# The first layer's stores moved to ScalarE's queue, and the next chunk's load one step earlier

## Chip, cores and metric
One core of a Trainium2 chip runs the whole program. The metric is the device time of one execution in microseconds (us), here the median of several runs. The program uses TensorE (PE: matrix multiplications), ScalarE (ACT) and VectorE (DVE) for everything elementwise, SyncE (SP) for nearly all transfers and GpSimd (POOL) for a few.

## What is computed
Three parts in a row: channel attention, which becomes a 256 x 256 matrix `a` that multiplies `v`, and two feed-forward layers on 6080 tokens with 256 channels and 2048 hidden ones.

```python
def _attn_ref(q, k, v, tau):
    qn = q / (np.linalg.norm(q, axis=1, keepdims=True) + 1e-06)
    kn = k / (np.linalg.norm(k, axis=1, keepdims=True) + 1e-06)
    s = kn.transpose(0, 2, 1) @ qn / tau
    ...
    return (v @ a).astype(np.float32)        # a: softmax of s over its last axis

def _moe_ref(x, w_in, w_out):                # first layer
    r = np.maximum(x @ w_in, 0.0)
    return ((r * r) @ w_out).astype(np.float32)

def _moe2_ref(x, w_in, w_out):               # second layer
    h = x @ w_in
    g = h * np.clip(h + 3.0, 0.0, 6.0) / 6.0
    return (g @ w_out).astype(np.float32)
```

The attention matrix is folded into the first layer's `w_in`, so after a head of about 100 us the kernel consists of two layers. Each multiplication takes three passes (high x high, high x low, low x high parts).

## The kernel before
**Chunks and steps.** The tokens are cut into six chunks of two blocks of 508 or 506 columns. A layer (`ph` 0 or 1) goes through its chunks (`c` 0 to 5), and a chunk through eight steps: four slices of the hidden channels (`u`), two halves each (`p`). `i` counts the steps over both layers, 0 to 95; `at` is the step within the chunk, 0 to 7 (`LAST`). In the trace chunk 1 of the first layer (i = 8 to 15) begins at 157.9 us, chunk 2 at 240.8, chunk 3 at 328.2, chunk 4 at 415.4, chunk 5 at 502.4, the second layer at 589.6; a step takes about 10.4 us.

**A step** (`step`, L669) multiplies by the input weights into PSUM (`mul`, L678, tile `s`), and ACT and DVE turn the sums into hidden values (copies `m`, `u`; values `h`; their high and low parts `g`). Between these multiplications TensorE does those by the output weights that belong to the step before (`out_mms`, run by `run_outs`, L662, tile `y`), 24 a step in portions (`pop`). The copy `m` of a step (L768) has to be done before the third group of `mul` (L783) may add into the same bank, and a copy `u` (L784) before the next (L790).

**Output tiles** (`y_done`, L645). With the last slice of a chunk its four sums (two blocks, two halves of the channels) are complete. As the output multiplications run one step late, this falls into step 0 of the next chunk: two of them in the middle of the step, two at its end. ACT copies each from PSUM into a tile `y` (L659; two buffers, `bufs=2`), and a store moves it to memory: to `scratch` (tensor `y` in the trace's names, so `y<-y`) for the first layer, to `outT` for the second. So the third eviction of a chunk needs the buffer of the first, whose store has to have landed.

**The next chunk's data** (`load_data`, L382) are two loads into the tile `blk`, which has one buffer. From it ACT and DVE make the operands `b`: the `lane`, filled by `add_lane` from the chunk's third step on, and at `LAST` for the rest; its last reader of `blk` is in the chunk's last step. The first layer loads from `vT`, the second from `scratch`; the data of the second layer's first chunk are loaded in chunk 5 of the first.

**Weights of the second layer** are converted during chunks 1 to 5 of the first layer by a planner (`background`): each task has a due step and is worked off in small pieces between a step's instructions (`beside`). A task loads raw words (`words`, L263, tile `w`), converts them on ACT (L135, L136: `ct<-w`, `cv<-w`) and DVE, and stores high and low parts (`keep`, L334: `w2h`, `w2l`, `o2h`, `o2l`).

**Order.** From i = 8 on each engine and queue takes its instructions in program order. SP's queue therefore holds, one behind the other as the program came to them: the words' loads, the stores of `keep`, the stores of `y`, the loads of `blk`. An issue waits on SP until its data are ready, and what is behind it waits too.

Of the kernel before, what the change touches and what calls it, by code (L numbers as in the profile page):

```python
# [59 lines left out]
def tile_channel_attention_then_two_ffn(  # L60
# [13 lines left out]
    PE, ACT, DVE, SP = nc.tensor, nc.scalar, nc.vector, nc.sync  # L74
# [125 lines left out]
    def run(fs):  # L200
        for f in fs:
            f()
# [16 lines left out]
    def add_task(name, load, due, alone=False, size=5):  # L219


        at = len(tasks)
        while at > 2 and tasks[at - 1].due > due:
            at -= 1
        tasks.insert(at, Task(name, load, due, alone, size))
        ensure_loads()
# [18 lines left out]
    def need(name):  # L245
        assert name in finished or any(t.name == name for t in tasks), name
        while name not in finished:
            background()
# [71 lines left out]
    def add_out_1(u, due):  # L320
        def parts(a):
            if (0, u) not in o_ops:
                o_ops[0, u] = [oop.tile([P, 4, C], F32R, tag="o" + t, name="o" + t) for t in "hl"]
            return [t[:, a:a + 2] for t in o_ops[0, u]]
        for a in (0, 2):
            add_task(("o", u) if a else None, convert_split(out_cut(w_out_1, u, a), 2, lambda a=a: parts(a)), due)
# [55 lines left out]
    def load_data(ph, c):  # L382
        r = blocks_tile("blk")
        data[ph, c] = r
        start, n = chunks[c]
        for g in range(2):
            src = vT[:, start + g * n:start + (g + 1) * n] if ph == 0 else scratch[c][:, g * n:(g + 1) * n]
            SP.dma_start(out=r[:, 2 * g:2 * g + 2, :n], in_=src.rearrange("(h p) t -> p h t", p=P))
# [16 lines left out]
    def add_lane(ph, c, slots, due):  # L405
        assert not lane
        b_ops.setdefault((ph, c), {})
        lane.extend(data_prep(data[ph, c], chunks[c][1], slots, new_slot(ph, c)))
        lane_due[0] = due

    def add_data(name, ph, c, slots, due):
        b_ops.setdefault((ph, c), {})
        add_task((name, ph, c), lambda: data_prep(data[ph, c], chunks[c][1], slots, new_slot(ph, c)), due,
                 size=2 * len(slots) + 2 * ("sums" in slots))
# [12 lines left out]
    def attn_w(u):  # L427

        if u == 1:

            ps = [psy.tile([P, 512], F32, tag=f"y0{dh}", name="aw") for dh in range(2)]
        else:
            ps = [bank([P, 512]) for _ in range(2)]

        def product(dh, eh):
            return lambda: PE.matmul(ps[dh], e_sb[dh][:, eh], w1[u][:, eh], start=(eh == 0), stop=(eh == 1))  # L436

        r = blocks_tile("wblk")
        data["w", u] = r

        def take(dh):
            def f():
                ACT.activation(out=r[:, dh:4:2], in_=ps[dh].rearrange("p (g f) -> p g f", g=2),
                               func=AF.Copy, scale=rsum[:, dh:dh + 1])
            return f
        return [product(dh, eh) for dh in range(2) for eh in range(2)], [take(dh) for dh in range(2)]
# [13 lines left out]
    with tc.tile_pool(name="qk", bufs=4) as qkp, tc.tile_pool(name="at", bufs=1) as atp:  # L460
# [53 lines left out]
        for i, (rest, j, g) in enumerate(pieces):  # L514
            if i:
                load_piece(i + 3)
            t = loaded[i]
# [86 lines left out]
    def in_1_steps(u):  # L604
        r = data["w", u]
        w_ops[0, u] = new_ops(wop, "w")
        ops = lambda: w_ops[0, u]
        if u < PLAIN:
            return split_slots(r, ops, RAW + OTHER)
        return split_slots(r, ops, RAW) + weight_sums(r) + split_slots(r, ops, SUMS)  # L610
# [8 lines left out]
    def out_mms(ph, c, u, p, g):  # L619


        n = chunks[c][1]
        wh, wl = o_ops[ph, u]
        first, last = (u, p) == (0, 0), (u, p) == (NU - 1, 1)
        mms = []

        def one(e, b, w, j, of, part, start, stop):
            def f():
                x = g[of][:, part, :n]
                if (ph, c, b, e) not in y_ps:  # L630
                    y_ps[ph, c, b, e] = psy.tile([P, HT], F32, tag=f"y{b}{e}", name="y")
                PE.matmul(y_ps[ph, c, b, e][:, :n], w[:, j, e * P:(e + 1) * P], x, start=start, stop=stop)  # L632
            return f


        for k, (i, b) in enumerate(((1, 1), (0, 1), (0, 0), (1, 0))):
            j = 2 * i + p
            for e in range(2):
                mms.append((one(e, b, wh, j, (i, b), 0, first and k % 2 == 0, False), None))
                mms.append((one(e, b, wl, j, (i, b), 0, False, False), None))  # L640
                mms.append((one(e, b, wh, j, (i, b), 1, False, last and k % 2 == 1),
                            (ph, c, b, e) if last and k % 2 else None))
        return mms

    def y_done(ph, c, b, e, last=False):  # L645
        start, n = chunks[c]
        if ph == 0 and c not in scratch:
            scratch[c] = dram.tile([C, 2 * HT], F32, tag="y1", name="y1")
        scale = 1.0 if ph == 0 else 1.0 / 6.0
        t = yp.tile([P, HT], F32, tag="y", name="y")  # L650
        y = y_ps[ph, c, b, e]
        dst = scratch[c][:, b * n:] if ph == 0 else outT[:, start + b * n:]
        dst = dst[e * P:(e + 1) * P]
        cuts = (0, n // 2, n) if last else (0, n)
        for k, (i, j) in enumerate(zip(cuts, cuts[1:])):
            if k:
                DVE.tensor_scalar(out=t[:, i:j], in0=y[:, i:j], scalar1=scale, scalar2=None, op0=ALU.mult)
            else:
                ACT.activation(out=t[:, i:j], in_=y[:, i:j], func=AF.Copy, scale=scale)  # L659
            SP.dma_start(out=dst[:, i:j], in_=t[:, i:j])  # L660

    def run_outs(outs, n):  # L662
        for _ in range(min(n, len(outs))):
# [148 lines left out]
    LAST = 2 * NU - 1  # L812
# [18 lines left out]
    for i, (ph, c, u, p) in enumerate(order):  # L831
        at = i % (LAST + 1)
        nxt = (ph, c + 1) if c + 1 < NCHUNK else (1, 0) if ph == 0 else None
        if ph == 0 and c == 0:
            if i == 0:
                add_out_1(1, 3)
            elif p == 1 and u + 1 < NU and u:
                add_out_1(u + 1, i + 2)
        if (ph, c) == (0, 1) and at == 0:
            end = i  # L840
            for x, f in [(x, f) for x in range(NU) for f in (add_in_2, add_out_2)]:
                end += DUE[f is add_out_2]
                f(x, end)
        if nxt and at == (1 if i > LAST else 3) + 1:
            add_lane(*nxt, FIRST, i - at + LAST)
        if at == 0:
            assert not lane
        if ph == 0:
            need(("w", ph, u))
            if PLAIN <= u and c == 0:  # L850
                need(("t", 0, 0))
            if c == 1 and u < PLAIN:
                need(("s", u))
        outs = []
        if not prev:
            need(("w1", 1))
            products, take = attn_w(1)
            outs = [(f, None) for f in products]
        else:
            if prev[0][0] == 0 and prev[0][1] == 0:  # L860
                need(("o", prev[0][2]))
            outs = out_mms(*prev[0], prev[1])
        if i == MANUAL_FROM:
            phase[0] = 2
            ctx.enter_context(tc.manual_schedule())

        if nxt and at == LAST:
            add_lane(*nxt, REST, i + 1)
        g, carry = step(i, ph, c, u, p, before, outs, carry)
        before = []  # L870
        if nxt and at == (1 if i > LAST else 3):
            load_data(*nxt)
        if ph == 0 and c == 0 and p == 0 and u + 1 < NU:
            need(("w1", u + 1))
            if u == 2:
                need(("s", 0))
            if u:
                products, before = attn_w(u + 1)
                run(products)
            else:  # L880
                before = take
            add_task(("w", 0, u + 1), lambda x=u + 1: in_1_steps(x), i + 2)
        if ph == 0 and c == 0 and u < PLAIN:
            if p == 0:
                add_data("t", 0, 0, ("sums", 5, 4, 3, 6), i + 2)
            else:
                add_weight_sums(u, SUMS_DUE)
        if ph == 0 and c == NCHUNK - 1 and p:
            fetch_2("w", u)
        if prev and prev[0][0] == 0 and prev[0][1] == NCHUNK - 1 and prev[0][3]:  # L890
            fetch_2("o", prev[0][2])
        prev = ((ph, c, u, p), g)
# [38 lines left out]
```

## Time and profile before
| | us |
|---|---|
| runs | 1091.4, 1099.7, 1102.7; median 1099.7 |
| profiled execution | 1099.3 |
| its span in the profile | 1097.5 |

| engine | busy us | share of the span |
|---|---|---|
| PE | 1071.4 | 98% |
| DVE | 900.3 | 82% |
| ACT | 648.8 | 59% |

The share of PE is an average over all stages, and matmuls that run at a lower clock count as busy too. So the stages have to be read one by one: how long each chunk takes, and at which granted clock. The rows of the section before the prediction give these, and the timelines of SP and ACT around the chunk ends.

### The profile page before, as it was taken

Reading aid. Unit: us, or ns where it says so; the run is one execution under the profiler, and the core shown is the slowest. Engines: PE = TensorE matmul, PEld = TensorE weight load, DVE = VectorE, ACT = ScalarE, POOL = GpSimd, SP = SyncE. Lnnn points to the kernel's source line nnn. Section 1 sums busy time; section 2 is a strip of 40 time slices with the busy share of each in tenths; the row PEclk is TensorE's granted clock in tenths of the full one; section 3 lists DMA queues with packets and bytes.
Section 4 is the critical chain, followed back from the end, with each engine's and each line's share of the span. In section 5 each row is a group of like instructions: output and inputs, shape, how many; then the busy total and the mean of one; then the engine's idle time right before and its main releaser. Section 6 shows DMA issues by size and latency. Waiting matters only on the chain.

```text
span 1097.5 us, 12762 instructions
## 1 busy us (share of the span) xinstructions
PE 1071.4 (98%) x4576; PEld 866.2 (79%) x4576; DVE 900.3 (82%) x1547; ACT 648.8 (59%) x1126; POOL 9.3 (1%) x22
## 2 busy tenths in 40 slices
PE   8999999999999999999999999999999999999998
PEld 6757778887887887888788888888888888888886
DVE  5899987886986886887677898898898898898785
ACT  5588966665566565667556545545545545555443
POOL 0000000000000000000101000000000000000000
PEclk9899999999999999999999999999999999999999
DMA  9523213114023014112544101100100100100001
GB/s 354 216 77 108 85 39 115 67 42 130 29 89 122 29 65 127 39 48 106 175 169 155 66 1 42 36 1 34 43 1 31 46 1 26 51 1 21 18 1 39
DMA packets 33568, 78.03 MB, mean 71 GB/s; under 512 B 3296, under 2 KB 16864, under 8 KB 33504
## 3 DMA queue, kind: packets, MB, share of 16 engines
q1 hardware_dynamic: 31200, 65.68, 17.7%
q0 software_dynamic: 2304, 11.54, 3.0%
q8 instruction: 36, 0.59, 0.2%
q14 instruction: 28, 0.23, 0.1%
HBM read 53.22 MB, written 23.99 MB: 70 GB/s over the span
## 4 chain that ended last, share of the span: by engine, by line
PE 88%; DVE 5%; DMA 3%; ACT 2%; issue 1%; SPq 1%; ACTq 0%; DVEq 0%
PE y L632 46%; PE s L683 40%; PE s L436 1%; DMA y<-y 1%; DVE accq L111 1%; DMA w<-w_in_dram 1%; DVE acck L111 1%; DMA blk<-vT_dram 1%; PE sc L505 1%; DMA blk<-y 1%; DVE g L108 0%; ACT sq L532 0%; DVE wl L108 0%; DMA w<-w_out_dram 0%; DVE b L108 0%
## 5 line engine op out<-in xcount | busy, mean ns | idle before, releaser
L632 PE MATMUL y<-g,oh 128*128 128x506 f32 (+1 forms) x1536 | 512.2, 394 | 0.3 <-ACT oh L105 0.3
L683 PE MATMUL s<-b,wh 128*128 128x506 f32 (+1 forms) x1348 | 423.3, 395 | 11.6 <-ACT u L105 5.5
L108 DVE TENSOR_TENSOR g<-h,g 128x506 fp32r<-128x506 f32 (+1 forms) x384 | 261.8, 682 | 108.3 <-ACT g L105 99.0
L632 PEld LDWEIGHTS y<-g,oh 128*128 128x128 f32 x1536 | 291.4, 190 | 66.2 <-ACT oh L105 0.8
L683 PEld LDWEIGHTS s<-b,wh 128*128 128x128 f32 x1348 | 253.9, 189 | 74.0 <-ACT u L105 7.9
L632 PE MATMUL y<-g,ol 128*128 128x506 f32 (+1 forms) x768 | 304.2, 396 | 0.3 <-DVE ol L108 0.2
L683 PE MATMUL s<-b,wl 128*128 128x506 f32 (+1 forms) x674 | 265.8, 394 | 0.6 <-DVE wl L108 0.6
L105 ACT ACTIVATE g<-h 128x506 fp32r<-128x506 f32 (+1 forms) x384 | 234.9, 622 | 27.0 <-DVE h L728 14.4
L105 ACT ACTIVATE u<-s 128x506 f32<-128x506 f32 (+1 forms) x188 | 111.6, 594 | 144.9 <-PE s L683 144.8
L632 PEld LDWEIGHTS y<-g,ol 128*128 128x128 f32 x768 | 145.7, 190 | 32.7 <-DVE ol L108 1.0
L111 DVE TENSOR_TENSOR h<-u,s 128x506 f32<-128x506 f32 (+1 forms) x188 | 127.5, 678 | 29.0 <-ACT u L105 27.7
L683 PEld LDWEIGHTS s<-b,wl 128*128 128x128 f32 x674 | 127.8, 190 | 29.6 <-DVE wl L108 1.6
L105 ACT ACTIVATE m<-s 128x506 f32<-128x506 f32 (+1 forms) x94 | 55.9, 595 | 111.8 <-PE s L683 111.4
L711 DVE SCALAR_TENSOR_TENSOR h<-r,h 128x506 f32<-128x506 f32 (+1 forms) x144 | 98.9, 687 | 4.9
L707 DVE SCALAR_TENSOR_TENSOR h<-h 128x506 f32<-128x506 f32 (+1 forms) x130 | 88.6, 681 | 1.4
L111 DVE TENSOR_TENSOR h<-m,s 128x506 f32<-128x506 f32 (+1 forms) x94 | 63.9, 680 | 15.0 <-ACT m L105 8.3
L727 ACT ACTIVATE r<-s,three 128x506 f32<-128x506 f32 (+1 forms) x48 | 32.9, 685 | 60.3 <-PE s L683 60.3
L710 DVE TENSOR_SCALAR r<-h 128x506 f32<-128x506 f32 (+1 forms) x144 | 60.5, 420 | 1.7
L108 DVE TENSOR_TENSOR b<-blk,b 128x506 fp32r<-128x506 f32 (+1 forms) x85 | 57.7, 679 | 0.0
L105 ACT ACTIVATE b<-blk 128x506 fp32r<-128x506 f32 (+1 forms) x85 | 52.5, 617 | 6.8 <-DMA blk<-vT_dram 3.5
L505 PE MATMUL sc<-q,k 128*128 128x256 f32 x192 | 47.8, 410 | 6.1 <-DMA q<-q_dram 6.1
L724 ACT ACTIVATE r<-s 128x506 f32<-128x506 f32 (+1 forms) x46 | 27.3, 594 | 43.2 <-PE s L683 42.9
(87 smaller groups left out, 478.3 us busy)
## 6 DMA issues: line engine op xcount, KB each, us to landing
w<-w_in_dram SPq DMA_DIRECT2D x16, 512.0 KB, 4.3
w<-w_out_dram SPq DMA_DIRECT2D x16, 512.0 KB, 3.8
k<-k_dram SPq DMA_DIRECT2D x10, 512.0 KB, 7.9
q<-q_dram SPq DMA_DIRECT2D x10, 512.0 KB, 8.8
blk<-vT_dram SPq DMA_DIRECT2D x8, 506.0 KB, 5.2
y<-y SPq DMA_DIRECT2D x16, 253.0 KB, 2.3
blk<-y SPq DMA_DIRECT2D x8, 506.0 KB, 5.2
outT_dram<-y SPq DMA_DIRECT2D x15, 253.0 KB, 2.1
```

Of the source, the lines that this page charges most:

```text
L105: ACT.activation(out=out, in_=in_, func=AF.Copy)
L108: DVE.tensor_tensor(out=out, in0=a, in1=b, op=ALU.subtract)
L111: DVE.tensor_tensor(out=out, in0=a, in1=b, op=ALU.add)
L436: return lambda: PE.matmul(ps[dh], e_sb[dh][:, eh], w1[u][:, eh], start=(eh == 0), stop=(eh == 1))
L505: return lambda: PE.matmul(s_ps[dh][:, :C], t["k"][:n, b, dh * P:(dh + 1) * P], t["q"][:n, b], start=first, stop=last)
L632: PE.matmul(y_ps[ph, c, b, e][:, :n], w[:, j, e * P:(e + 1) * P], x, start=start, stop=stop)
L683: PE.matmul(dst, w[:, a, rows], x, start=first and k == 0, stop=k == 2, skip_group_check=True)
L707: DVE.scalar_tensor_tensor(out=h, in0=h, scalar=0.0, in1=h, op0=ALU.max, op1=ALU.mult)
L710: DVE.tensor_scalar(out=r, in0=h, scalar1=3.0, scalar2=0.0, op0=ALU.add, op1=ALU.max)
L711: DVE.scalar_tensor_tensor(out=h, in0=r, scalar=6.0, in1=h, op0=ALU.min, op1=ALU.mult)
L724: ACT.activation(out=r, in_=x, func=AF.Relu)
L727: ACT.activation(out=r, in_=x, func=AF.Relu, bias=three)
```

## The change
Three lines. The store of an output tile of the first layer is issued by ACT, right behind ACT's own eviction; the second layer's stay on SP. From i = 8 on `load_data` is called after a chunk's first step and no longer after its second. The condition of `add_lane` is written in another way.

```diff
@@ y_done
-            SP.dma_start(out=dst[:, i:j], in_=t[:, i:j])
+            (ACT if ph == 0 else SP).dma_start(out=dst[:, i:j], in_=t[:, i:j])
@@ main loop
-        if nxt and at == (1 if i > LAST else 3) + 1:
+        if nxt and at == (2 if i > LAST else 4):
             add_lane(*nxt, FIRST, i - at + LAST)
...
         g, carry = step(i, ph, c, u, p, before, outs, carry)
         before = []
-        if nxt and at == (1 if i > LAST else 3):
+        if nxt and at == (0 if i > LAST else 3):
             load_data(*nxt)
```

## Rows read from the trace of the kernel before

**Rows 1.** Windows (us; busy PE, PEld, DVE, ACT, POOL; clock): chunk 1, chunks 2-5, next.

```profile
157.87:240.75 82.88, 82.88 (x361) 67.64 (x361) 67.25 (x114) 54.06 (x96) 0.00 (x0) 1.00 0.22 73
240.75:589.61 348.86, 338.69 (x1442) 275.98 (x1441) 266.83 (x446) 211.18 (x375) 7.42 (x14) 0.98 0.28 92
589.61:672.60 82.99, 82.99 (x362) 67.66 (x361) 72.10 (x123) 43.87 (x75) 1.16 (x3) 1.00 0.18 60
```

**Rows 2.** Waits of TensorE: us in total, times, longest us.

```profile
PE s L683 <- ACT u L105: 5.5, 3, 2.6
PE s L683 <- ACT m L105: 5.1, 2, 2.6
```

**Rows 3.** Windows, columns as in rows 1: the stretch after the first stall.

```profile
256.56:260.70 4.14, 4.14 (x11) 3.30 (x12) 2.87 (x5) 2.79 (x5) 0.00 (x0) 0.60 1.00 302
```

**Rows 4.** Timeline of ACT, chunk 2 (start us, us, instruction, idle before and releaser).

```profile
246.60 1.08 ACT L659 ACTIVATE y<-y 128x508 f32<-128x508 f32 x2
...
254.73 1.29 ACT L659 ACTIVATE y<-y 128x508 f32<-128x508 f32 x2 [4.25 <-DMA y<-y]
```

**Rows 5.** Timeline of SP, chunk 2; the last line holds four issues.

```profile
248.77 0.32 SPq L334 DMA_DIRECT2D o2l<-stl  x1
249.18 0.39 SPq L263 DMA_DIRECT2D w<-w_in_dram  x1
249.66 6.70 SPq L660 DMA_DIRECT2D y<-y  x4
```

**Rows 6.** Timeline of SP, end of chunk 2 and chunk 3.

```profile
326.22 0.42 SPq L263 DMA_DIRECT2D w<-w_in_dram  x1
...
346.51 0.32 SPq L334 DMA_DIRECT2D o2l<-stl  x1
346.88 0.42 SPq L263 DMA_DIRECT2D w<-w_in_dram  x1
347.36 0.97 SPq L388 DMA_DIRECT2D blk<-vT_dram  x2
```

**Rows 7.** Timelines of DVE and ACT, end of chunk 2 and chunk 3.

```profile
325.74 0.68 DVE L108 TENSOR_TENSOR b<-blk,b 128x506 fp32r<-128x506 f32 x1
...
350.77 0.66 ACT L135 ACTIVATE ct<-w 128x512 f32<-128x512 f32 x1
354.91 0.62 ACT L105 ACTIVATE b<-blk 128x506 fp32r<-128x506 f32 x1 [3.49 <-DMA blk<-vT_dram]
```

**Rows 8.** Issues (ns min/median/max) of L660 and L388; L660's landings at 247 to 258.

```profile
L660 SPq DMA_DIRECT2D y<-y x24: 319/320/422, 164.3 to 600.7; - x24
...
L388 SPq DMA_DIRECT2D blk<-y x12: 377/476/1205, 521.1 to 933.2; - x12
...
DMA to landing us min/median/max: 2.0/3.6/5.2
```

**Rows 9.** Timelines of ACT and PE, chunk 1, undisturbed.

```profile
163.69 1.07 ACT L659 ACTIVATE y<-y 128x508 f32<-128x508 f32 x2
165.28 0.59 ACT L724 ACTIVATE r<-s 128x508 f32<-128x508 f32 x1 [0.51 <-PE s L683]
...
167.58 1.29 ACT L659 ACTIVATE y<-y 128x508 f32<-128x508 f32 x2
168.96 0.60 ACT L105 ACTIVATE m<-s 128x508 f32<-128x508 f32 x1
...
170.83 0.63 PE L683 MATMUL s<-b,wh 128*128 128x508 f32 x2
```

**Rows 10.** Timelines of SP and ACT, chunk 5.

```profile
506.71 0.43 SPq L263 DMA_DIRECT2D w<-w_out_dram  x1
508.83 4.88 SPq L660 DMA_DIRECT2D y<-y  x4
521.10 1.72 SPq L388 DMA_DIRECT2D blk<-y  x2
...
512.08 1.28 ACT L659 ACTIVATE y<-y 128x506 f32<-128x506 f32 x2
```

## Prediction

> **What bounds the kernel now.** I read the times by stage first. In chunk 1 of the first layer TensorE is busy for the whole 82.88 us of the chunk, at a granted clock of 1.00; the next four chunks together take 348.86 us, with 338.69 busy [rows 1]. Four chunks like chunk 1 would take 4 x 82.88 = 331.52 us. So 348.86 - 331.52 = **17.3 us** is lost there, and the reader should ask where. The chunks of the second layer run like chunk 1 (the first of them 82.99, [rows 1]), so nothing of this size is lost later.
>
> The waits of TensorE come next. It waits for an ACT copy `m` twice (5.1 us) and for an ACT copy `u` three times (5.5 us), with 2.6 us as the longest of each [rows 2]: four waits of about 2.5 us, and a small one. Each costs more than its idle time: after the first, TensorE ran 4.14 us at a granted clock of 0.60 [rows 3], that is at the lower of its two levels (1.2 GHz) for most of the stretch. That is 4.14 x 0.40 = 1.7 us more, so some 4.3 us a stall, and four of them make 17.1 us, close to the 17.3.
>
> Then the reason for each, from the timelines of SP and ACT. There are two kinds.
>
> *Kind one, chunks 2 and 4: a store is late.* In chunk 2 ACT evicted two output tiles from 246.60 to 247.68, but SP issued the first store only at 249.66 [rows 4, 5]: ahead of it stood a weight store that could leave at 248.77 and a weight load at 249.18. SP takes its instructions in order. Tile `y` has two buffers, so the third eviction waits for the first store to land: ACT stood still for 4.25 us, until 254.73 [rows 4], and with it the copy `m` behind. Chunk 4 repeats it; these are the two waits for `m`.
>
> *Kind two, chunks 3 and 5: a load is late.* In chunk 3 the load of the next data stands behind a weight store that left at 346.51 and leaves at 347.36 [rows 6], and ACT's first instruction on it waits 3.49 us, to 354.91 [rows 7], with the copy `u` behind it. In chunk 5 the load leaves at 521.10 [rows 10].
>
> **The change, part by part.** *L844* is rewritten to the same value (`at` 2 or 4): nothing changes there.
>
> *L871, the load one step earlier.* Ten `load_data` calls move in program order. For the second layer nothing is issued on SP between the end of a chunk's first step and the end of its second, so its order of instructions, and its time, stay as they are. In the first layer five calls (in chunks 1 to 5) pass what the second step puts on SP: in chunk 3 one pair of weight stores and one weight load, in chunk 5 one pair of stores. In chunk 3 the load can then leave once SP has issued the weight load at 326.22 and DVE has read the old block for the last time (325.74 + 0.68 = 326.42) [rows 6, 7], so at 326.7 where it left at 347.36. There it was landed 7.6 us after it left (354.91, [rows 7]); 326.7 + 7.6 = 334.3, and ACT wants it at 351.4, right after 350.77 + 0.66. Cover: 17 us. In chunk 5 it can leave at 507.2, behind the weight load at 506.71 [rows 10]: 13.9 us before 521.10, where the wait of this kind in chunk 3 was 3.49 us. Both stalls of kind two go. Behind the load on SP stands the second step's first weight store, some 17 us later in chunk 3 (it leaves a little before the 346.51 of its pair), so nobody waits for the load's issue.
>
> *L660, 24 stores from ACT.* Six chunk ends, four stores each. In chunks 2 and 4 a store can leave as its eviction ends: 246.60 + 0.60 = 247.2 in place of 249.66. Stores of this window landed 2.0 to 5.2 us after issue, the slow one right behind the weight load [rows 8]; now it leaves 2 us ahead of that load, so I take 2.0 to 3.6 (the median): landed by 250.8. ACT reaches the third eviction at 254.73 - 4.25 = 250.5 [rows 4], plus what the two issues cost it. Both stalls of kind one go. All four gone: **-17.3 us**.
>
> The price is ACT's time. No row shows ACT issuing a transfer. The nearest are SP's issues of the same stores, 319 to 422 ns; the slowest issue on SP is 1205 ns, of a load [rows 8]. Call e an issue with its wait for the eviction ahead of it (ACT's later instructions wait behind it). Chunk 1 shows the slack, undisturbed [rows 9]. Eviction one starts at 163.69. With two issues the next instruction could start at 163.69 + 2 x 0.60 + 2e = 164.89 + 2e where it started at 165.28: 2e - 0.39 late. What follows runs without a gap to eviction three (167.58), then come two more issues: eviction three at 167.19 + 2e, the copy `m` at 168.39 + 4e, done at 168.99 + 4e. TensorE needs it at 170.83 [rows 9]. So nothing is lost up to e = (170.83 - 168.99) / 4 = **0.46 us**. I take 0.42, the slowest row of the same transfer: 0 us. Below, e = 0.32 is 0 too; above, e = 1.2 gives 4 x 1.2 - 1.84 = 2.96 us in each of six chunks.
>
> *What is late next.* In chunk 5 the earlier load meets the stores: weight load at 506.71, the two halves of the block from about 507.2 to 508.2, and store one at 508.8. If it lands in 5.2 us, as behind the weight load of chunk 2 [rows 8], it lands at 514.0; eviction three is due at 512.08 + 2e - 0.39 = 512.5 [rows 10], so it is 1.5 us late, with 4 x (0.46 - 0.42) = 0.2 us of slack left: 1.3 us of stall. If it lands in 3.6 us, nothing. Bounds 0 to 1.3 + 1.7 of slow clock = 3.0; I take the slower landing without the clock, 1.3. In chunk 3 the load has landed (334.3) before the stores leave (334.6). In chunks 2 and 4 ACT's next reader is of the weight load issued at 249.18: the like load, issued at 346.88 with a block load behind it, was there by 350.77, in under 3.9 us [rows 6, 7]; 253.1 is before ACT comes to it (`m` done at about 253.6). Nothing.
>
> *The sum.* The profiled execution took 1099.3 us (span 1097.5 and 1.8 around it); the median of the three runs is 1099.7, the lowest 1091.4. 1099.3 - 17.3 + 1.3 = **1083.3 us**; I say 1083. Whichever execution is looked at, the stalls are a matter of landings, so the lowest run may well have had two fewer; the changed kernel should then spread less.
>
> **A rule against it.** The rows show a store that was ready at 247.2 and left at 249.66 because of what stood ahead of it on SP [rows 4, 5]; its own issue is 0.32 us [rows 8]. The Trainium skill, "DMA: Bandwidth & Descriptors", section "Issuing engines are not separate DMA queues", says that transfers started by different engines end on the same 16 DMA engines and interleave, and that starting them from several engines saves only the time to start them. By that rule L660 would save no more than a few issues, and the two stalls of kind one would stay. I weigh the rows higher, since the wait ahead of the issue is on SP and not on the DMA engines; no row shows two queues' transfers of this size side by side at a store.
>
> **The rivals.**
> 1. *The stores stay late* (they share the DMA engines with the weight load and, now, the block load). For it: the 5.2 us landing. Against it: the store leaves 2 us ahead of the weight load. Half the loss stays: 1099.3 - 8.7 = 1090.6 us.
> 2. *No gain:* the new issues on ACT and collisions in chunks 3 and 5 give the whole back, or the stalls were this execution's alone. Against it: four stalls with a named cause each. About 1098 us.
> 3. *Slower:* ACT's issue is dear. It decides from the point where six stalls outweigh 17.3 us, 2.9 a chunk: e = 0.46 + 2.9 / 4 = 1.2 us without a fall of the clock, and with 1.7 us for the clock e = 0.76. At e = 1.2 with the clock: 6 x (2.96 + 1.7) = 28 us, 1099.3 - 17.3 + 28 = 1110 us. Against it: SP's issues of this very store never passed 0.42.
> 4. *The load doesn't move:* excluded for chunks 3 and 5, since SP's order shows what stands ahead of it; for chunk 1 and the second layer it holds, and is worth nothing.
>
> **Chances and range.** Forecast (all four go, 1077 to 1088): 0.63. Rival 1 (1086 to 1094): 0.17. Rival 2 (1094 to 1104): 0.12. Rival 3 (1100 to 1115): 0.08. The low end allows 6 us for runs whose head or landings are better than those of the profiled one (the lowest run before lies 8 under it); the high end takes in rival 1 and the edge of rival 2, so that 2 in 10 are left out: 1077 to 1095. A measurement of this kernel can tell about 1% from no change, so the bounds are 1088.7 and 1110.7. Faster: 0.63 and half of rival 1, 0.72. Slower: the dear part of rival 3, 0.06. Between them: the rest, 0.22.
>
> **What would show each step.** Chunks 2 to 5 at about 82.9 us each, TensorE at clock 1.00 in all of them; no wait of ACT's eviction for a store over 1.5 us; no wait of ACT for a block. ACT-queue issues of 0.3 to 0.45 us, and the copy `m` of a chunk's second step done before TensorE wants it. I am wrong if these issues take 0.6 us or more, if chunk 5 stalls as before at its stores, or if a weight load becomes what ACT waits for.

## Result and profile after

The changed kernel took 1082.4 us in the median of four runs (1080.4 to 1089.8), the kernel before 1095.9 in the median of its four (1091.4 to 1102.7): the ratio is 0.986, 95% interval 0.981 to 0.991, so 1.4% faster. Two later comparisons, each beside the kernel before on one chip, gave 0.987 (0.982 to 0.991; 1082.8 against 1099.4 us) and 0.984 (0.981 to 0.986; 1081.3 against 1098.4 us).

The windows of the profiled execution (1080.4 us, span 1078.6), chunks 1 to 5 of the first layer and the first chunk of the second; columns as in [rows 1]:

```profile
154.74:237.63 82.89, 82.89 (x361) 67.64 (x361) 67.36 (x114) 53.98 (x96) 0.00 (x0) 1.00 0.18 61
237.63:320.65 83.02, 83.02 (x361) 67.99 (x361) 68.64 (x116) 53.45 (x95) 0.00 (x0) 1.00 0.26 81
320.65:403.39 82.74, 82.74 (x362) 68.10 (x361) 67.35 (x115) 54.15 (x96) 0.00 (x0) 1.00 0.23 78
403.39:486.11 82.72, 82.72 (x362) 67.83 (x361) 67.94 (x115) 53.95 (x96) 0.00 (x0) 1.00 0.23 73
486.11:571.40 85.29, 83.16 (x361) 67.70 (x361) 63.08 (x103) 50.05 (x88) 7.46 (x14) 1.00 0.46 154
571.40:654.40 83.00, 83.00 (x362) 67.66 (x361) 72.08 (x123) 43.84 (x75) 1.21 (x3) 1.00 0.17 57
```

The last line is that of the chunk that the change was not to touch (82.99 in [rows 1]), and it did not. Chunks 2 to 4 now run as chunk 1 does, TensorE busy all the time at a granted clock of 1.00. Chunk 5 kept 2.1 us of idle time. Together chunks 2 to 5 take 83.02 + 82.74 + 82.72 + 85.29 = 333.8 us where they took 348.86 [rows 1]: 15.1 us less. The two profiled executions differ by 18.9 us; the other 3.8 are no work of the change: chunk 1 begins 3.1 us earlier (154.74 against 157.87), mostly because the execution of before ran at a lower granted clock in its head (0.94 from 50 to 100 us, where the other has 1.00), and 0.7 us lie in the second layer.

TensorE's waits after (us in total, times, longest), which answer to [rows 2]:

```profile
PE s L683 <- ACT m L105: 2.1, 1, 2.1
...
PE s L683 <- ACT u L105: 0.4, 1, 0.4
```

In place of four stalls there is one, and it is another: in chunk 5 TensorE waited for a copy `u` before, and now it waits for `m`. How ACT lives with its new instructions shows in the timeline of ACT in chunk 1, beside [rows 9]:

```profile
160.56 0.59 ACT L659 ACTIVATE y<-y 128x508 f32<-128x508 f32 x1
161.18 0.35 ACTq L660 DMA_DIRECT2D y<-y  x1
161.58 0.59 ACT L659 ACTIVATE y<-y 128x508 f32<-128x508 f32 x1 [0.42 <-ACT y L659]
162.20 0.33 ACTq L660 DMA_DIRECT2D y<-y  x1
162.57 0.59 ACT L724 ACTIVATE r<-s 128x508 f32<-128x508 f32 x1 [0.40 <-ACT y L659]
...
166.80 0.60 ACT L105 ACTIVATE m<-s 128x508 f32<-128x508 f32 x1 [0.40 <-PE s L683]
```

From eviction to eviction 161.58 - 160.56 = 1.02 us pass, of which 0.60 is the eviction: an issue costs ACT 0.42 us, 0.03 before it, 0.33 to 0.35 for itself, and some 0.05 until the next instruction starts. It is 0.40 for the second of the pair and 0.46 after the third store and in some other places; the mean of the chunk's four is 0.42. The copy `m` is done at 167.40; TensorE wants it 12.96 us after the chunk's begin (170.83 - 157.87 in [rows 9, 1]), so at 167.70. It is in time by 0.3 us, and TensorE does not stop.

The remaining stall is in chunk 5. First the timeline of SP there, beside [rows 10]:

```profile
490.45 0.43 SPq L263 DMA_DIRECT2D w<-w_out_dram  x1
490.92 1.01 SPq L388 DMA_DIRECT2D blk<-y  x2
```

then that of ACT:

```profile
491.94 0.59 ACT L659 ACTIVATE y<-y 128x506 f32<-128x506 f32 x1
492.56 0.33 ACTq L660 DMA_DIRECT2D y<-y  x1
...
498.66 0.59 ACT L659 ACTIVATE y<-y 128x506 f32<-128x506 f32 x1 [2.39 <-DMA y<-y]
```

and the landing times of the four stores L660 from 489 to 502:

```profile
DMA to landing us min/median/max: 2.0/3.8/6.0
```

The block load left at 521.10 before, long after the stores [rows 10]; now it leaves 1.6 us ahead of the first one (490.92 and 492.56), right behind a weight load (490.45). That store takes 6.0 us to land, and the third eviction waits 2.39 us for its buffer.

### The profile page after: what moved, and what is told of

Read it like the earlier page. It is cut to its first block, busy times and chain, and to the rows that moved or that the text cites. A ratio compares the mean times of both kernels' runs of the same rounds, so it can differ in the third digit from the quotient of the medians.

```text
span 1078.6 us, 12754 instructions
## 1 busy us (share of the span) xinstructions
PE 1062.4 (98%) x4576; PEld 861.3 (80%) x4576; DVE 900.6 (83%) x1547; ACT 649.1 (60%) x1126; POOL 9.4 (1%) x22
## 3 DMA queue, kind: packets, MB, share of 16 engines
q1 hardware_dynamic: 27744, 59.45, 16.6%
## 4 chain that ended last, share of the span: by engine, by line
PE 91%; DVE 4%; DMA 2%; ACT 1%; issue 1%; SPq 0%; ACTq 0%
PE y L632 48%; PE s L683 41%; PE s L436 1%; DMA w<-w_in_dram 1%; DVE accq L111 1%; DMA y<-y 1%; DVE acck L111 1%; DVE g L108 1%; DMA q<-q_dram 0%; DVE wl L108 0%; ACT sq L532 0%; PE sc L505 0%; DVE b L108 0%; DMA w<-w_out_dram 0%; SPq L486 0%
```

## The experiments

No run leaves any work out; each was compared with the kernel before on the same chip.

**Theory:** there are two kinds of stall, each cured by its own part of the change, and the new stall of chunk 5 comes from the block load beside the stores. **Rivals:** starting the stores from another engine saves only the time to start them, so kind one would stay; or the earlier load only moves its stall; or the weight load alone delays chunk 5's store; or ACT has so much idle time that its issues could not cost anything.

**Stores alone** (from the kernel before).

```diff
-            SP.dma_start(out=dst[:, i:j], in_=t[:, i:j])
+            (ACT if ph == 0 else SP).dma_start(out=dst[:, i:j], in_=t[:, i:j])
```

> The first-layer stores on ACT alone, the loads where they were. Theory (each part cures its own kind of stall): chunks 2 and 4 run at about 82.9 us, chunks 3 and 5 keep their waits for the block at about 87.2 us each; 8.7 us less than before, ratio 0.992. Chunk 5 has no wait of an eviction for a store over 1 us, since no block load stands beside the stores. Rival (starting transfers from another engine saves only the time to start them): chunks 2 and 4 stay near 87 us and the ratio is 1.00.

Measured: 1091.2 us against 1099.4, ratio 0.9935 (0.9904 to 0.9967). Windows of chunks 2 to 5:

```profile
238.95:321.98 83.03, 83.03 (x362) 68.00 (x361) 68.65 (x116) 53.43 (x95) 0.00 (x0) 1.00 0.26 81
321.98:410.31 88.33, 84.59 (x362) 69.14 (x361) 67.50 (x115) 54.00 (x96) 0.00 (x0) 0.98 0.22 73
410.31:493.18 82.87, 82.87 (x361) 67.74 (x361) 67.94 (x115) 53.92 (x96) 0.00 (x0) 1.00 0.22 73
493.18:579.01 85.83, 83.26 (x361) 67.73 (x361) 63.02 (x103) 49.87 (x88) 7.43 (x14) 1.00 0.44 153
```

Chunks 2 and 4 are cured, chunks 3 and 5 are not. ACT still waits for the block there:

```profile
ACT b L105 <- DMA blk<-vT_dram: 4.6, 1, 4.6
ACT b L105 <- DMA blk<-y: 3.4, 1, 3.4
```

Where 87.2 us each were expected they take 88.33 and 85.83; in the second of them the clock did not fall (1.00). In chunk 5 the first stores, with no block load beside them, land in 2.0 to 2.5 us. The rival falls: what ACT's queue saves is the wait on SP behind a weight store, far more than the issue. With it the store also leaves ahead of the weight load, behind which one of chunk 2's stores had taken 5.2 us to land [rows 8]; the run does not part the two.

**The earlier load alone** (from the kernel before).

```diff
-        if nxt and at == (1 if i > LAST else 3):
+        if nxt and at == (0 if i > LAST else 3):
             load_data(*nxt)
```

> The earlier load alone, all stores on SP. Theory: the load now stands behind the four stores on SP but ahead of the second step's weight stores; it leaves at about 340 in chunk 3 and 514 in chunk 5 and has landed before ACT wants it, so chunks 3 and 5 run at about 82.9 us; chunks 2 and 4 keep the wait of an eviction for a store, about 87.2 us each; 8.7 us less than before, ratio 0.992. Rival (the earlier load only moves the stall into the stores): chunk 5 stays above 85 us.

Measured: 1086.4 us against 1099.4, ratio 0.990 (0.986 to 0.994). Windows of chunks 2 to 5:

```profile
237.67:323.61 85.94, 83.30 (x361) 67.91 (x361) 68.66 (x116) 53.21 (x95) 0.00 (x0) 1.00 0.24 78
323.61:406.34 82.73, 82.73 (x361) 68.08 (x361) 67.26 (x115) 53.98 (x96) 0.00 (x0) 1.00 0.25 78
406.34:493.31 86.97, 84.53 (x362) 68.91 (x361) 68.04 (x115) 53.96 (x96) 0.00 (x0) 0.98 0.21 70
493.31:576.32 83.01, 83.01 (x361) 67.81 (x361) 62.96 (x103) 49.91 (x88) 7.43 (x14) 1.00 0.45 155
```

The mirror image: chunks 3 and 5 cured, 2 and 4 not. Here the block load stands behind the four stores on SP and disturbs none of them in chunk 5, as the timeline of SP shows:

```profile
499.76 4.88 SPq L660 DMA_DIRECT2D y<-y  x4
504.70 0.98 SPq L388 DMA_DIRECT2D blk<-y  x2
```

Nothing has moved into the stores. The medians differ by 13.0 us where 8.7 were expected. In the profile chunks 2 to 5 take 10.2 us less than before, as chunk 2 kept its clock (1.00), and the head is 3.1 us shorter, which the change does not touch.

**The changed kernel beside its parts.** No edit.

> The changed kernel once more, beside the parts. Theory: three stalls gone, chunk 5 keeps one of about 2 us idle at its stores (window of about 85.3 us); ratio 0.984 to 0.988. Rival (the stall of chunk 5 was that one execution's): chunk 5 at about 82.9 us in this profile.

Measured: 1082.8 us against 1099.4, ratio 0.987 (0.982 to 0.991). Chunk 5, and in it the stretch right after the stall:

```profile
486.89:573.75 86.86, 84.69 (x361) 68.84 (x361) 63.05 (x103) 49.89 (x88) 7.43 (x14) 0.98 0.45 151
502.00:506.50 4.50, 4.33 (x13) 3.49 (x14) 3.16 (x5) 2.30 (x6) 0.00 (x0) 0.63 0.19 72
```

The stall of chunk 5 is there again, with a wait of TensorE of 2.2 us and a wait of the third eviction of 2.42 us. Here the clock fell after it (0.63 in the stretch shown), as it had not in the first profile, and the chunk took 86.86 us, more than the 85.3 expected. The two parts gave 0.65% and 1.0%, together 1.7%, and the whole change 1.35%. The intervals (0.3 to 0.4% to each side) are too wide to read anything from that difference. The windows show where the whole is less than the sum: in chunks 2 to 5 the profiles of the parts save 8.8 and 10.2 us, this one of the whole 13.5, and 3.9 us are the stall of chunk 5 at its stores, which neither part alone has.

**The load ahead of a chunk's first step** (from the changed kernel).

```diff
+        if nxt and i > LAST and at == 0:
+            load_data(*nxt)
         g, carry = step(i, ph, c, u, p, before, outs, carry)
         before = []
-        if nxt and at == (0 if i > LAST else 3):
+        if nxt and i < LAST and at == 3:
             load_data(*nxt)
```

> The changed kernel with the block load issued ahead of a chunk's first step, so ahead of that step's weight load on SP. Theory (in chunk 5 the store shares the DMA engines with the block load): the block load leaves at about 478 to 484, has landed before the stores, the third eviction of chunk 5 waits less than 0.5 us, and chunk 5 runs at about 82.9 us; 2.4 us less than the changed kernel. Rival (the weight load ahead of the store is enough to delay it): the third eviction of chunk 5 still waits 2 us and the time is that of the changed kernel.

Measured: 1078.6 us against 1099.4 (the changed kernel, on that chip, 1082.8), ratio 0.984 (0.979 to 0.989). Chunk 5's window:

```profile
485.70:568.69 82.99, 82.99 (x362) 67.82 (x361) 63.02 (x103) 49.88 (x88) 7.50 (x14) 1.00 0.47 157
```

The timeline of SP around its begin:

```profile
483.80 0.88 SPq L388 DMA_DIRECT2D blk<-y  x2
...
490.06 0.43 SPq L263 DMA_DIRECT2D w<-w_out_dram  x1
```

The timeline of ACT, first store and third eviction:

```profile
492.16 0.33 ACTq L660 DMA_DIRECT2D y<-y  x1
...
495.72 0.57 ACT L659 ACTIVATE y<-y 128x506 f32<-128x506 f32 x1
```

The landing times of the stores L660 from 488 to 500:

```profile
DMA to landing us min/median/max: 2.0/2.2/2.6
```

The weight load still leaves 2.1 us ahead of the first store (490.06 and 492.16), as in the changed kernel; only the block load is gone from there (483.80), and the store lands in 2.6 us at most. The third eviction starts without a wait, chunk 5 loses nothing, and no stall is left in chunks 2 to 5. So the weight load alone does not make the store late, and the rival falls: the block load has to come to it. Whether the block load alone would do it, no run shows.

**The same and the changed kernel once more, on another chip.**

> The block load ahead of a chunk's first step once more, beside the changed kernel. Theory: 2.4 us and more under the changed kernel, ratio to before 0.981 to 0.986. Rival: the difference of the first look lies in the head of the program alone, and the two come out within 1 us of each other.

> The changed kernel beside the two others. Theory: chunk 5 at about 85.3 us in this profile too, ratio to before 0.984 to 0.988. Rival: as above, within 1 us of the kernel with the load ahead of the first step.

Measured: 1081.1 us (1078.4 to 1085.1, six runs) with the load ahead of the first step, 1081.3 us (1080.2 to 1084.1, five runs) for the changed kernel; ratios to before 0.983 (0.980 to 0.986) and 0.984 (0.981 to 0.986). The profiles show the stall of chunk 5 in the changed kernel again (TensorE waits 2.3 us, and the clock did not fall) and none in the other; their spans were 1079.1 and 1076.8 us. Chunk 5 of the changed kernel:

```profile
486.46:571.92 85.46, 83.20 (x361) 67.70 (x361) 63.05 (x103) 50.03 (x88) 7.46 (x14) 1.00 0.46 153
```

The medians do not separate the two here: the 2.4 us that were expected are in the profiles, not in the medians. Of the six executions with the load ahead of the first step, the four longer ones (1080.7 to 1085.1 us) have a mean granted clock of 0.994 to 0.997 and the two shorter ones 0.999; the longer ones have no profile of their own, and where the clock was lost in them stays open. That the stall is gone is shown; that the kernel is faster by it is not. It is seen on one chip of two, in three executions of four (1078.4 to 1078.7 us against 1082.4 and more; the fourth took 1085.0).

**Two issues behind each eviction** (from the kernel with the load ahead of the first step).

```diff
-            (ACT if ph == 0 else SP).dma_start(out=dst[:, i:j], in_=t[:, i:j])
+            mid = (i + j) // 2
+            for lo, hi in ((i, mid), (mid, j)) if ph == 0 else ((i, j),):
+                (ACT if ph == 0 else SP).dma_start(out=dst[:, lo:hi], in_=t[:, lo:hi])
```

> The kernel with the block load ahead of a chunk's first step, and each first-layer store cut into two halves, both issued by ACT: two issues behind each eviction. Theory (the slack behind the evictions ends at a cost of 0.46 us an eviction): the two issues cost 0.42 + 0.33 + 0.04 = 0.79 us, the copy m of a chunk's second step is late by 4 x 0.79 - 1.84 = 1.3 us at each of six chunk ends; chunks 2 to 5 at about 84.2 us, some 8 us more than with whole stores, more if the clock falls. Rival (ACT has room for them, its busy share being 60%): chunks 2 to 5 stay at 82.9 us and the time at that of whole stores.

Measured: 1094.9 us against 1098.4, ratio 0.9965 (0.9944 to 0.9986); 13.8 us slower than with whole stores. TensorE's longest group of waits:

```profile
PE s L685 <- ACT m L105: 12.1, 6, 2.5
```

The first of its places, in the timeline of PE:

```profile
169.63 0.73 PE L685 MATMUL s<-b,wh 128*128 128x508 f32 x2 [1.55 <-ACT m L105]
```

The timeline of ACT in chunk 1:

```profile
160.78 0.59 ACT L659 ACTIVATE y<-y 128x508 f32<-128x508 f32 x1
161.41 0.83 ACTq L662 DMA_DIRECT2D y<-y  x2
162.28 0.60 ACT L659 ACTIVATE y<-y 128x508 f32<-128x508 f32 x1 [0.91 <-ACT y L659]
...
168.98 0.59 ACT L105 ACTIVATE m<-s 128x508 f32<-128x508 f32 x1 [0.89 <-ACT y L659]
```

Two issues cost 162.28 - 160.78 - 0.60 = 0.90 us an eviction, 0.11 more than expected: the pair of issues alone takes 0.83, where one takes 0.33. With 0.90 the prediction's slack gives 4 x 0.90 - 1.84 = 1.76 us of lateness a chunk; TensorE waited 1.55 in chunk 1 and 12.1 in six places, 2.0 on the mean. The expected 8 us became 14 to 15, because e was larger, two evictions waited for stores as well (3.7 us), and in one of the chunks the clock fell (0.98 over the 83 us from 239.63). ACT is busy for 59% of the span and still had no room for a second issue at this place: the rival falls.

## Why the prediction was right

**The two kinds of stall** held, each with its cause and its cure. The three stalls that were to go in chunks 2 to 4 went as a whole: 83.02, 82.74 and 82.72 us where the prediction had about 82.9.

**The order on SP** held: only in chunks 3 and 5 does the load pass a weight transfer, and in the second layer nothing changed (571.40 to the end takes 507.2 us, 507.9 before). In chunk 3 the load leaves at 319.20, 1.4 us before the chunk begins (320.65); predicted from [rows 6, 7] was 1.5 before it.

**The price of ACT's issues** held. Taken was 0.42 us, the slowest issue of the same store on SP; measured is 0.40 to 0.46 us, 0.42 on the mean of chunk 1. That the figures agree is in part luck, since it is made up otherwise: an issue of 0.33 and 0.07 to 0.13 around it. The slack of 0.46 us is borne out from both sides: at 0.42 TensorE does not wait, at 0.90 it waits 1.55 us in chunk 1 where the slack gives 1.76.

**What is late next** was the right place and mechanism; the term was too small. Predicted was 1.3 us in chunk 5, from a landing of 5.2 us. The store landed in 6.0 to 6.1 us, so the stall was 2.1 to 2.3 us of idle time, and chunk 5 took 85.29, 86.86 and 85.46 us in the three profiles of the changed kernel, where it takes 82.99 without the stall: 2.3, 3.9 and 2.5 us. The first and the last lie inside the bounds of 0 to 3.0; the middle one, with the fall of the clock, does not. The row from which the term was taken, a store behind a weight load in one queue, was the nearest, but it had one load of 512 KB ahead of it, and in chunk 5 a weight load of that size and two halves of the block of 508 KB each are ahead. Two of the prediction's own signs failed with this term: chunk 5 is not at about 82.9 us, and an eviction waits more than 1.5 us for a store. It had also named a stall of chunk 5 at its stores as a sign of being wrong, though its own sum held one of 1.3 us.

In chunks 2 and 4 the prediction looked at the weight load and not at the block load, which leaves among the stores there too. The line of SP in chunk 2, and the landing times of that chunk's stores:

```profile
246.51 0.99 SPq L388 DMA_DIRECT2D blk<-vT_dram  x2
```

```profile
DMA to landing us min/median/max: 2.0/4.4/6.8
```

It leaves between the second store (245.10) and the third (248.27). Stores of chunks 2 and 4 took up to 6.8 and 7.2 us, and nothing was lost: the third and the fourth eviction did not wait for a store, so the late ones were among the last two, whose buffers nobody needs until the next chunk's end.

**The sum** was 17.3 - 1.3 = 16.0 us for chunks 2 to 5; measured are 15.1 in the first pair of profiles, and 13.5, 16.6 and 17.1 us between the medians of the three comparisons. That the time came out as 1082.4 where 1083 was predicted is in part luck: the prediction set out from one execution of 1099.3 us, and the median of the four before is 1095.9. The head plays into it too, in which the profiled execution of before had lost 3 us that the changed one did not.

**The rule against it.** The Trainium skill, "DMA: Bandwidth & Descriptors", section "Issuing engines are not separate DMA queues", agrees with the runs in one half and not in the other. That transfers from different engines interleave on the same DMA engines agrees with chunk 5: a store from ACT took 6.0 us beside SP's block load and at most 2.6 us without it. That several issuing engines save only the time to start the transfers does not agree with chunks 2 and 4: the issue takes 0.32 us, and what was saved is a wait of 2.5 us in SP's order and with it a landing behind the weight load, 2.9 to 4.2 us of the chunk (85.94 and 86.97 with the stores on SP, 83.03 and 82.7 to 82.9 with them on ACT).

**The spread.** It did shrink: 1080.2 to 1084.1 and 1082.4 to 1084.1 us in the two later comparisons, against 1090.9 to 1106.1 for the kernel before; in the first one it was 1080.4 to 1089.8 against 1091.4 to 1102.7. With the load alone it was 1085.8 to 1088.1 (four executions), with the stores alone 1088.2 to 1097.5 (ten), which suggests that the wide spread goes with the late block load, but does not show it. That the lowest run of before had two stalls fewer, as the prediction supposed, is not shown, for only the execution of 1099.3 has a profile. A lesser fall of the clock would nearly do: the shortest execution of the later comparisons (1090.9 us) has a mean granted clock of 0.996 and the profiled one 0.990, which is some 6.6 of the 8.4 us between them (an estimate: 0.006 of 1097.5). What one stall costs does differ: in the kernel with the load alone 2.6 us of idle time cost chunk 2 no more than 2.9 us (granted clock of the chunk 1.00), and 2.4 us cost chunk 4 4.2 (0.98); in the changed kernel the stall of chunk 5 cost 2.3, 3.9 and 2.5 us.

## What to carry to other kernels

A store that is ready but stands behind another transfer's wait is late by that wait, and it pays to issue it where its data are made, if the engine there has room for the issue at that very place: count the issue as 0.42 us of that engine, not as nothing, and look at the slack behind it, not at its busy share. When a load is moved to an earlier place, look at which short stores leave just then and whether somebody waits for one of them: beside the first store of chunk 5 the load cost a stall, beside the last ones of chunks 2 and 4 nothing. A step earlier or later on the same queue can decide that.

## What the runs showed of the hardware

- An issue on ACT takes 326 ns (median of 24), hardly more than the 320 on SP, but the next ACT instruction starts some 0.04 to 0.10 us after it, and an issue that waits for the eviction ahead of it takes away the overlap of two evictions: a pair took 1.07 us back to back [rows 9] and takes 2.0 us to the next instruction with the issues.
- A 253 KB store that takes 2.0 us by itself took 6.0 us on a queue of its own beside a block load of two times 508 KB from another queue, which had left 1.6 us ahead of it, and a weight load of 512 KB just ahead of that; beside the weight load without the block load it took at most 2.6 us.
- Two issues in a row on ACT took 0.81 to 0.83 us, more than twice the 0.33 of one.
- The same idle time of TensorE, 2.4 to 2.6 us, lowers the granted clock in one place and not in another of one execution (chunks 4 and 2 of the kernel with the load alone). It does so at one and the same place too: in chunk 5 of the changed kernel the clock fell after 2.2 us in one execution, and not after 2.1 and 2.3 us in two others.
